# A causal five-tap convolution in 64x64 quadrants instead of shifted copies, in an attention and gated-unit kernel

## The chip, the cores and the metric

The kernel runs on one core of a Trainium2 chip. The metric is the device time of one execution in microseconds (us). A core has five engines that run side by side and wait for each other only through semaphores: TensorE (PE, matrix products into PSUM; PEld are its weight loads), VectorE (DVE), ScalarE (ACT), GpSimd (POOL) and SyncE (SP), which here only issues transfers. Sixteen DMA engines move the data.

## The reference

Attention over chosen chunks of keys, followed by a gated linear unit. For 4 batches, 8 heads, 768 positions and head size 64:

```python
k_min, k_max = k_chunks.min(3), k_chunks.max(3)         # 24 chunks of 32 keys
ub = sum_d max(q*k_min, q*k_max)                        # a bound for each query and chunk
ub = where(chunk is not later than the query's, ub, -1e9)
top = the 6 chunks with the largest ub
scores = where(key in a chosen chunk and not later than query, q@k.T / 8, -1e9)
x = softmax(scores) @ v          # then x is [4, 768, 512], heads side by side
gate = sigmoid(sum_k conv_w[k] * x shifted by 4-k positions)   # 5 taps, each channel alone
out = (gate * (x @ w_val)) @ w_out
```

## The kernel before, in words

Two heads make a pair, 128 channels; there are 16 pairs, four to a batch. Every pair goes through the same stages, in two halves of 384 positions where a PSUM bank (512 floats to a partition) asks for it:

- `load`: K, Q and V of the pair, in float32, rows of 64 floats. `tr` transposes K and Q on TensorE (L462), `kev` and `qev` copy them to float16 (`Kh`, `Qh`).
- `kred` takes the maximum and minimum over each chunk, `ksmall` (L493 to L499) makes the small matrix `KB` from them: the chunk values less those of the first chunk, in a high and a low float16 part, each head in its own half of the partitions. `KB` is zeroed once, by the operations `kbz`, so that one head's columns don't meet the other's rows.
- `qlo` makes the low part of Q; `rhi` and `rlo` the positive parts. `ub` (L547) sums four products for each of five blocks of 128 queries, 96 columns each: 24 chunks, two heads, two terms.
- `bsum`, `top`, `cmp` find the sixth largest bound and mark what is below it, `selT` transposes the marks (L587), `mcopy` copies them to `MT`.
- `score` (L606, L611) multiplies keys and queries of the two heads in the two halves of the array's rows, and adds the penalty for chunks not chosen; `exps` (L620) takes the exponential, `tri` (L628) clears what is above the diagonal.
- `av` (L649) multiplies by V with a column of ones, `norm` divides, `toxT` (L674) transposes the result and `xcopy` stores it as `xT`: channels on partitions, positions along the row with four zeros before.
- the convolution. `xw` (L684) writes `xT` to a scratch area in DRAM as 32 rows of four channel groups, and `xs` (L690) reads it back four times into `XS`, two of the four copies shifted by three positions. A partition of `XS` then holds a channel of every group, and `conv` (L707) makes 32 channels at a time, three column offsets with weights `WD`, in four column strips of the array, the four copies serving for the taps and for the high and low part of the weights. The last pair doesn't go through DRAM: it takes ten full matmuls a half with diagonal weights `WF` (L700). `w_split` and `w_diag` make `WD`, `l_split` and `l_diag` make `WF`, on VectorE and GpSimd, in the start.
- `tanh` (L713) makes the gate, and at the end of a batch `val` (L732), `gated` (L740), `outmm` (L756), `outev` (L766, L763) and `outdma` make the output.

The order of the work is written out before anything runs. `graph` lists all operations with the engine, an assumed duration, what they read and write and which PSUM banks they hold; `Graph.schedule` plays this through and, on an engine that is free, starts the ready operation with the smallest key:

```python
def key(stage, p, x=0.0):
    return p * period + off[stage] + off.get((stage, p), 0.0) + x
```

The offsets `OFF` (by stage) and `DELTA` (by stage and pair) set the priorities. The order that comes out is the order of the instructions on each engine, and each engine keeps it on the chip, so an instruction that waits holds up those behind it on its engine. SyncE issues loads, scratch transfers and output in one such queue. `NBUF` says how many buffers a stage has; `XS` has three of 6,192 B a partition.

Of the kernel before, what the change touches and what calls it, by code (L numbers as in the profile page):

```python
# [47 lines left out]
for _bi, _segs in enumerate(BANKS):  # L48
    for _col, _jt, _q0, _n in _segs:
        for _i in range(_n // 128):  # L50
# [3 lines left out]
            MT=2, on=2, xT=8, XS=3, g=8, gv=8, osb=4, scr=4)  # L54

PERIOD = 13.8602
OFF = dict(wbig=1148.236, cw=125.765, load=358.845, ktr=-336.423, qtr=-37.679, kev=406.626, qev=-139.346,
           ksm=-456.212, spl=623.116, vc=107.062, ub=-495.797, top=132.081, selT=-719.785, sc=-163.548,
           ex=-132.526, av=74.786, nrm=-290.402, tox=-288.094, xs=-175.045, conv=-212.494, tanh=-65.208,
           val=282.113, gv=294.749, out=-225.697, ev=-231.055)  # L60
# [3 lines left out]

DELTA = dict(
    wbig=(-4.147, -9.138, 14.054, 16.549, 24.22, 23.981, -3.255, -6.784, -8.585, -2.745, 13.034, 0, -24.136,
        -9.796, 0, 3.457),
    cw=(0, 89.865, 2.841, 1.73, -0.853, 3.445, 0, 7.465, 3.491, 0, -27.97, 1.384, -15.849, 36.25, -0.166,
        -20.384),
    load=(2.212, 2.245, 11.447, 7.343, 5.77, 0, 21.497, 8.567, -0.48, -11.783, -22.651, -40.845, -3.315,  # L70
        -5.727, -1.703, -8.004),
    ktr=(0, -2.634, 4.621, 8.626, 0.714, 0, 7.232, -2.689, -0.185, 4.209, -4.073, 0, 4.296, 0, 15.148, -5.02),
    qtr=(-15.204, 1.215, 0.818, 1.874, -8.456, -4.665, 3.458, -9.187, -23.627, 0.086, -14.556, 178.494, -3.223,
        14.633, -145.093, 7.271),
    kev=(11.876, -5.688, -9.671, 8.56, -7.116, 0, 12.665, 0.619, -15.123, -13.007, -10.166, -6.817, 6.199,
        -3.806, -0.155, -1.266),
    qev=(37.149, 2.471, -16.182, 10.459, 29.657, -0.249, -3.69, 9.604, -0.818, 2.696, -1.078, 12.98, -4.017,
        5.163, 5.476, 5.435),
    ksm=(0, -4.38, 5.046, 9.366, -11.093, -1.908, 3.385, -3.157, -13.805, 2.514, -0.981, 0, 1.21, 4.081,
        11.674, 10.127),  # L80
    spl=(0.346, -24.171, -2.279, -4.139, -5.56, -6.293, 12.646, 0.444, 0, -3.044, 0.73, 2.081, -5.907, -1.059,
        -2.827, -3.273),
    vc=(17.191, 3.409, 9.445, 3.878, -0.963, 0.335, 1.042, -2.48, 4.91, 5.77, 4.98, -4.793, 2.229, -17.202,
        -0.574, -2.167),
    ub=(13.662, 0, 0, 0, -8.33, -0.206, 0, 3.499, 3.993, -0.744, -2.331, 15.574, 26.827, 28.804, 16.738, 22.841),
    top=(25.292, -24.694, 4.497, -2.001, 1.256, 0, 16.093, 20.425, 0.505, -0.792, 0.187, 5.136, 4.425, 0.403,
        15.388, 11.54),
    selT=(-1.809, 13.447, 1.899, 2.153, -2.029, 27.133, 0.995, -4.451, -1.013, 1.728, 3.47, 2.835, 5.548,
        -1.394, -3.599, -4.491),
    sc=(-9.568, -6.679, 5.526, 4.615, -3.539, -11.917, -0.459, -1.374, 9.815, -3.896, 14.566, -29.319, 8.563,  # L90
        30.742, -5.263, -5.85),
    ex=(-15.686, -3.542, 41.162, 0, 8.566, 12.219, 4.858, -2.833, -10.993, 3.823, 16.222, 17.001, 13.392,
        -7.227, -1.623, -6.598),
    av=(-5.142, 0, -0.433, 0, 2.631, -5.212, 0, -5.273, 3.957, -3.38, 21.214, 11.344, 0.382, 2.169, -2.023,
        -2.85),
    nrm=(3.682, -5.189, 0, 0.178, -1.097, -13.888, 0, 4.991, 1.934, 0.324, 17.742, 0, 0, 0, 2.094, 5.151),
    tox=(0, 0.806, -0.064, 4.178, 10.744, -13.609, -5.142, -5.072, 0.301, 13.148, 1.471, -2.4, 16.567, 3.615,
        10.288, 0),
    xs=(0.835, -6.145, 0, -2.707, -15.901, -3.535, -0.514, 15.609, -2.935, -5.898, -7.227, -6.339, -7.872,
        2.836, -17.515, -1.283),  # L100
    conv=(1.109, -9.317, -7.864, 1.674, 14.425, 10.565, -18.213, 12.768, -35.205, -0.311, 0.911, -3.335, 4.553,
        0.715, -2.444, -81.052),
    tanh=(2.328, -10.547, 0.619, -51.267, -16.342, 0, 1.062, 25.583, 15.578, 4.988, -1.56, -26.423, -22.742,
        -18.959, 4.891, 1.516),
    val=(6.813, -1.57, 4.188, 7.508, 0, -26.519, -2.852, -6.757, 6.641, -4.111, -1.579, 0.052, 10.772, 5.618,
        -1.442, 3.684),
    gv=(2.408, -10.058, -23.155, -50.121, -16.673, -7.413, -28.068, -2.821, 0, -0.313, -1.153, 5.876, 2.097,
        5.659, -0.953, -3.286),
    out=(2.159, -7.291, 5.362, -0.981, 12.886, 0, -0.946, 13.16, 0, 18.939, 0.187, 0, 4.861, 24.141, 16.05,
        24.703),  # L110
    ev=(0.036, 2.704, 13.217, 11.95, 16.092, 5.482, 5.301, 2.521, -1.154, -11.056, -34.733, -21.796, -10.2,
        19.865, -1.415, 6.277),
# [163 lines left out]
def act(n):  # L276
    return 0.051 + n / 1200.0
# [14 lines left out]
def graph(off, period, nbuf):  # L292
# [34 lines left out]
    def c_zero(i):  # L327
        return lambda: t.nc.vector.memset(t.tiles["KB"][i], 0.0)
    for i in range(2):
        G.op(f"kbz{i}", "DVE", 0.2, -190, c_zero(i), w=[("KBz",)])  # L330
# [37 lines left out]
    def w_cw():  # L368
        t.nc.sync.dma_start(out=t.cw, in_=t.conv_w.rearrange("k (c d) -> (k c) d", d=32))
    G.op("cw", "SP", 0.6, key("cw", 1), w_cw, w=[("cw",)], lat=3.0)  # L370
# [6 lines left out]
    def w_rep():  # L377
        t.nc.vector.tensor_copy(out=t.cw4, in_=t.cw.unsqueeze(2).to_broadcast([80, 32, 4]))
    G.op("cwrep", "DVE", 0.6, 11.4, w_rep, r=[("cw",)], w=[("cw4",)])

    def w_tr():
        t.nc.tensor.transpose(out=bank("cwT")[:, 0:80], in_=t.cw4.rearrange("p d b -> p (d b)"),
                              identity=t.ident[0:80, 0:80])
    G.op("cwT", "PE", 0.12, 11.4, w_tr, r=[("cw4",), ("ident",)], ps=["cwT"])

    def w_split():
        nc, b = t.nc, bank("cwT")
        v, c4 = nc.vector, t.ident.rearrange("p (c b) -> p c b", b=4)
        v.tensor_reduce(out=t.pm[:, 0:4], in_=t.ident.rearrange("p (c b) -> p b c", b=4), axis=AX.X, op=ALU.add)
        v.tensor_reduce(out=t.id4, in_=c4, axis=AX.X, op=ALU.add)  # L390
        v.tensor_tensor(out=t.pm[:, 4:6], in0=t.pm[:, 0:2], in1=t.pm[:, 2:4], op=ALU.add)
        v.tensor_tensor(out=t.pm[:, 6:7], in0=t.pm[:, 0:1], in1=t.pm[:, 1:2], op=ALU.add)
        v.tensor_tensor(out=t.pm[:, 7:8], in0=t.pm[:, 2:3], in1=t.pm[:, 3:4], op=ALU.add)
        v.tensor_copy(out=t.whi, in_=b[:, 0:80])
        v.tensor_tensor(out=t.wlo, in0=b[:, 0:80], in1=t.whi, op=ALU.subtract)
        v.tensor_scalar(out=t.wlo, in0=t.wlo, scalar1=t.pm[:, 5:6], scalar2=None, op0=ALU.mult)
        v.scalar_tensor_tensor(out=t.wlo, in0=t.whi, scalar=t.pm[:, 4:5], in1=t.wlo, op0=ALU.mult, op1=ALU.add)
        v.tensor_scalar(out=t.wsel, in0=t.wlo[:, 0:48], scalar1=t.pm[:, 6:7], scalar2=None, op0=ALU.mult)
        v.scalar_tensor_tensor(out=t.wsel[:, 0:32], in0=t.wlo[:, 48:80], scalar=t.pm[:, 7:8], in1=t.wsel[:, 0:32],
                               op0=ALU.mult, op1=ALU.add)  # L400
    G.op("wsplit", "DVE", 2.7, 11.4, w_split, r=[("cwT",), ("ident",)], w=[("wsel",)], ps=["cwT"],
         after=[G.ops[-1]])

    def w_diag(j):
        def emit():
            sl = slice(12 * j, 12 * j + 12)
            t.nc.gpsimd.tensor_tensor(
                out=t.WD[:, sl, :], in0=t.id4.unsqueeze(1).to_broadcast([128, 12, 32]),
                in1=t.wsel[:, sl].unsqueeze(2).to_broadcast([128, 12, 32]), op=ALU.mult)
        return emit  # L410
    for j in range(4):
        G.op(f"wdiag{j}", "POOL", 0.8, 12.3 + 0.1 * j, w_diag(j), r=[("wsel",)], w=[("WD",)])


    def l_dma():
        t.nc.sync.dma_start(out=t.cl, in_=t.conv_w[:, DM - 128:DM])
    G.op("cl", "SP", 0.5, key("cw", 3), l_dma, w=[("cl",)], dma=0.1)

    def l_tr():
        t.nc.tensor.transpose(out=bank("clT")[:, 0:KSZ], in_=t.cl, identity=t.ident[0:KSZ, 0:KSZ])  # L420
    G.op("clT", "PE", 0.1, key("cw", 5), l_tr, r=[("cl",), ("ident",)], w=[("clT",)], ps=["clT"])

    def l_split():
        v, b = t.nc.vector, bank("clT")
        v.tensor_copy(out=t.lh, in_=b[:, 0:KSZ])
        v.tensor_copy(out=t.lw[:, 0:KSZ], in_=t.lh)
        v.tensor_tensor(out=t.lw[:, KSZ:2 * KSZ], in0=b[:, 0:KSZ], in1=t.lh, op=ALU.subtract)
# [480 lines left out]
```

The softmax here doesn't subtract the row's maximum and nothing guards it: scores larger than these inputs give would overflow.

## Time and profile before

| | |
|---|---|
| time, median of 3 runs | 226.72 us (225.72 to 227.03) |
| span of the profiled execution | 226.8 us |
| mean granted TensorE clock | 0.932 |
| PE, DVE, ACT, POOL busy | 86%, 68%, 63%, 44% |
| moved by DMA | 41.53 MB, 183 GB/s |
| XS<-scr | 60 transfers of 193.3 KB |
| scr<-xT | 15 transfers of 193.5 KB |
| K, Q, V | 80 transfers, 18.4 MB |

The page gives busy time by engine, the span in 40 slices (a digit is tenths; PEclk is the clock that TensorE was granted), the chain of work that ended last, the costliest groups of instructions by line and shape, and the transfers. Other views answer for a stretch of time: busy time by stretch, the chain or the instructions in order of time, and who waited for whom. A busy share alone doesn't tell what a change is worth; the chain and the stretches do.

### The profile page before, as it was taken

What the parts mean: (1) busy time and instruction counts of PE and PEld (TensorE: products, weight loads), DVE (VectorE), ACT (ScalarE), POOL (GpSimd) and SP (SyncE); (2) the same over time, 40 slices, a digit from 0 to 9 for tenths busy, and PEclk for the clock granted to TensorE, in tenths of its full rate; (3) what the DMA queues carried; (4) which work ended last, traced back from release to release, by engine and by line L of the source; (5) the groups of instructions that cost most, each with busy time, mean ns of one, the idle gap of its engine ahead of it and who ended that gap; (6) DMA issues with size and microseconds to landing.
All of it is one profiled execution on the core that took longest, in us unless ns stands there. A gap on an engine that the chain in (4) does not pass through costs nothing.

```text
span 226.8 us, 7127 instructions
## 1 busy us (share of the span) xinstructions
PE 195.6 (86%) x2710; PEld 131.4 (58%) x2710; DVE 155.1 (68%) x495; ACT 141.9 (63%) x310; POOL 99.1 (44%) x219
## 2 busy tenths in 40 slices
PE   7355999999995899993999996986999999939993
PEld 2255777858664768561586783562665658515441
DVE  4989899979986388985198896694576547203252
ACT  2313796996996458695589943793899881231421
POOL 8799886487183324358047613443163410000000
PEclk9857699999999589999699999997999999997999
DMA  5999998788858996898599699787143007674333
GB/s 122 220 218 219 151 208 175 176 179 238 218 137 195 242 269 139 193 265 281 131 211 254 154 231 260 160 281 251 35 143 134 9 7 198 197 259 150 139 137 140
DMA packets 84519, 41.53 MB, mean 183 GB/s; under 512 B 76545, under 2 KB 79494, under 8 KB 84486
## 3 DMA queue, kind: packets, MB, share of 16 engines
q1 hardware_dynamic: 83430, 40.04, 72.1%
q0 software_dynamic: 1056, 1.05, 3.1%
q8 instruction: 21, 0.34, 0.6%
q14 instruction: 12, 0.10, 0.1%
HBM read 32.86 MB, written 9.26 MB: 186 GB/s over the span
## 4 chain that ended last, share of the span: by engine, by line
PE 63%; DMA 11%; DVE 7%; POOL 5%; SPq 5%; ACT 4%; issue 2%; ACTq 0%; DVEq 0%; POOLq 0%
DMA XS<-scr 9%; PE b L732 8%; PE b L606 8%; PE b L756 8%; PE b L649 8%; PE b L707 8%; PE b L462 7%; PE b L611 6%; SPq L690 5%; PE b L547 5%; ACT P L620 4%; POOL WF L433 3%; PE b L587 2%; PE b L674 2%; DMA qn<-in_q_dram 2%
## 5 line engine op out<-in xcount | busy, mean ns | idle before, releaser
L620 ACT ACTIVATE P<-b 128x512 f16<-128x512 f32 (+2 forms) x192 | 89.8, 598 | 17.0 <-PE b L611 12.0
L628 POOL TENSOR_SCALAR_AFFINE_SELECT P<-P 128x512 f16<-128x512 f16 (+1 forms) x64 | 34.4, 557 | 39.3 <-ACT P L620 38.5
L606 PE MATMUL b<-Qh,Kh 64*128 64x128 f16 (+3 forms) x384 | 41.0, 267 | 0.1
L611 PE MATMUL b<-MT,E 64*128 64x128 f16 (+4 forms) x352 | 37.5, 263 | 0.0
L474 DVE TENSOR_REDUCE km<-b 128x12 f32<-128x384 f32 x64 | 32.8, 549 | 3.6 <-PE b L462 2.8
L740 DVE SCALAR_TENSOR_TENSOR gv<-g,b 128x384 f16<-128x384 f32 x32 | 17.5, 550 | 24.2 <-PE b L732 21.7
L707 PE MATMUL b<-XS,WD 128*32 128x384 f16 x360 | 20.5, 364 | 13.2 <-DMA XS<-scr 12.9
L713 ACT ACTIVATE g<-b 128x384 f32<-128x384 f32 x32 | 15.3, 503 | 24.0 <-PE b L707 15.8
L649 PE MATMUL b<-VA,P 128*128 128x65 f16 x672 | 29.1, 198 | 0.0
L649 PEld LDWEIGHTS <-P 128*128 128x128 f16 x672 | 26.0, 100 | 3.7 <-issue 1.9
L606 PEld LDWEIGHTS <-Kh 64*128 64x128 f16 x384 | 18.5, 96 | 13.6 <-issue 8.9
L732 PE MATMUL b<-xT,wval 128*128 128x384 f16 x128 | 24.8, 332 | 0.0
L504 ACT ACTIVATE Qh<-b 128x384 f16<-128x384 f32 x32 | 15.9, 548 | 12.6 <-PE b L462 12.3
L766 ACT ACTIVATE osb<-b 128x512 f32<-128x512 f32 x21 | 12.9, 613 | 16.6 <-PE b L756 16.4
L536 POOL CAST VA<-vn 128x768 f16<-128x768 f32 x16 | 13.3, 838 | 22.3 <-DMA vn<-in_v_dram 11.6
L756 PE MATMUL b<-wout,gv 128*128 128x512 f16 x96 | 22.7, 379 | 0.0
L468 ACT ACTIVATE Kh<-b 128x384 f16<-128x384 f32 x32 | 16.0, 545 | 9.8 <-PE b L462 8.7
L707 PEld LDWEIGHTS <-WD 128*32 128x32 f16 x360 | 9.1, 103 | 21.8 <-issue 15.7
L611 PEld LDWEIGHTS <-E 64*128 64x128 f16 x352 | 17.7, 97 | 4.2 <-issue 1.1
L462 PE MATMUL b<-ident,qn 128*128 128x128 f32 x96 | 17.0, 308 | 3.0 <-DMA qn<-in_q_dram 3.0
L462 PE MATMUL b<-ident,kn 128*128 128x128 f32 x96 | 15.5, 301 | 4.7 <-DMA kn<-in_k_dram 2.8
L658 DVE TENSOR_TENSOR on<-b,rcp 128x384 f16<-128x384 f32 x32 | 17.8, 558 | 1.1
(82 smaller groups left out, 328.9 us busy)
## 6 DMA issues: line engine op xcount, KB each, us to landing
XS<-scr SPq DMA_DIRECT2D x60, 193.3 KB
kn<-in_k_dram SPq DMA_DIRECT2D x32, 192.0 KB
qn<-in_q_dram SPq DMA_DIRECT2D x32, 192.0 KB
vn<-in_v_dram SPq DMA_DIRECT2D x16, 384.0 KB
out_dram<-osb SPq DMA_DIRECT2D x24, 256.0 KB
scr<-xT SPq DMA_DIRECT2D x15, 193.5 KB
wval<-in_moe_w_val_dram POOLq DMA_DIRECT2D x1, 512.0 KB, 8.1
wout<-in_moe_w_out_dram POOLq DMA_DIRECT2D x1, 512.0 KB, 10.5
```

The costliest lines, as they stand in the source:

```text
L462: t.nc.tensor.transpose(out=b[:, j * 128:(j + 1) * 128], in_=vv(name, p)[:, 3 * w + j, :], identity=t.ident)
L474: t.nc.vector.tensor_reduce(out=vv("km", p)[:, i, w * 12:(w + 1) * 12], in_=bank(("kn", p, w))[:, 0:HB].rearrange("p (c t) -> p c t", t=CH ...
L606: nc.tensor.matmul(out=bb[hh][:, col:col + n], lhsT=kh[HP[hh], jt * 128:(jt + 1) * 128], rhs=qh[HP[hh], q0:q0 + n], start=(si == 0), stop= ...
L611: nc.tensor.matmul(out=bb[hh][:, col + m0 - q0:col + n], lhsT=t.E[HP[hh], jt * 128:(jt + 1) * 128], rhs=mt[HP[hh], m0 - 128:q0 + n - 128], ...
L620: t.nc.scalar.activation(out=t.P[p % 2][hh][bi], in_=bank(("s", p, bi, hh))[:, 0:n], func=AF.Exp, scale=0.125 / QS)
L628: t.nc.gpsimd.affine_select(out=ap, in_=ap, pattern=[[0, n], [1, 128]], compare_op=ALU.is_ge, fill=0.0, base=0, channel_multiplier=-1)
L649: t.nc.tensor.matmul(out=b[:, qt, :], lhsT=t.P[p % 2][hh][bi][:, col:col + 128], rhs=vv("VA", p)[:, hh, jt, :], start=(jt == 0), stop=(jt ...
L658: t.nc.vector.tensor_tensor(out=vv("on", p)[:, :, hh * 64:(hh + 1) * 64], in0=b[:, :, 0:D], in1=rc.unsqueeze(2).to_broadcast([128, NT, D]) ...
L707: t.nc.tensor.matmul(out=b[32 * g:32 * g + 32, 0:HB], lhsT=t.WD[:, o * 16 + (p % 4) * 4 + g, :], rhs=x[:, g * XW + w * HB + o:g * XW + w * ...
L732: t.nc.tensor.matmul(out=k[:, 0:HB], lhsT=t.wval[:, ct, et * 128:(et + 1) * 128], rhs=t.xT[:, (4 * b_ + ct) % 8, 4 + w * HB:4 + (w + 1) * HB],
L740: t.nc.vector.scalar_tensor_tensor(out=vv("gv", 4 * b_ + et)[:, sl], in0=vv("g", 4 * b_ + et)[:, sl], scalar=1.0, in1=bank(("val", b_, et, ...
L756: t.nc.tensor.matmul(out=k, lhsT=vv("gv", 4 * b_ + et)[:, s * 128:(s + 1) * 128], rhs=t.wout[:, et, :], start=(et == 0), stop=(et == NCT - 1))
```

## The change

The convolution is done in quadrants of the array. A quadrant multiplies 64 channels (half of the partitions) by a 64x64 diagonal weight and writes 64 channels. The two halves of positions are computed at the same time: the first half of the rows (channels 0 to 63 of `xT`) makes positions 0 to 383 and the second half of the rows (channels 64 to 127) makes positions 384 to 767. For what remains, a copy `XQ` of `xT` has the two halves of the partitions swapped. Ten steps (five taps, high and low part of the weight) of four matmuls make a pair, all of them one operation that holds both PSUM banks. Two transfers inside SBUF make `XQ`; scratch area and shifted copies are gone, and the last pair is treated like the others. The weights `WQ` are built in the start, from conv_w as 40 rows of 64, in place of `WD` and `WF`.

The bounds stream only chunks that a block of queries can see: of the four products the first keeps all 24 chunks and clears the bank, the others take 4i+8 (i is the block's number). `ksmall` works on both heads at once, with a mask `hm` that also carries the scale, so `KB` is written whole and isn't zeroed in advance.

In the start, TensorE's planned gaps before 26 us are filled with products of a zero tile (`fill`), and for pairs 0 and 1 `rhi` and `mcopy` go from VectorE to ScalarE.

Assumed transfer times in the planner, PERIOD, OFF and DELTA change too, so the order of all stages is another one. `val` must come after the convolution of its channels.

```diff
-            MT=2, on=2, xT=8, XS=3, g=8, gv=8, osb=4, scr=4)
+            MT=2, on=2, xT=8, XS=3, XQ=3, g=8, gv=8, osb=4, scr=4)
+EARLY = (0, 1)
+FILL, FILL_MM = 26.0, 0.3
+CONV = "QQQQQQQQQQQQQQQQ"
...
-            t.nc.vector.memset(t.tiles["KB"][i], 0.0)
+            t.nc.vector.memset(t.hm[HP[hh], hh, :], QS)
+            t.nc.vector.memset(t.hm[HP[hh], 1 - hh, :], 0.0)
...
+        def q_diag(k):
+            def emit():
+                for m in range(2):
+                    t.nc.gpsimd.tensor_tensor(
+                        out=t.WQ[:, m, k], in0=t.id2.unsqueeze(1).to_broadcast([128, 8, 64]),
+                        in1=t.qw[:, m, 8 * k:8 * k + 8].unsqueeze(2).to_broadcast([128, 8, 64]), op=ALU.mult)
...
-            e.tensor_scalar(out=ks, in0=ks, scalar1=QS, scalar2=None, op0=ALU.mult)
-            for hh in range(2):
-                hp, cs = HP[hh], slice(hh * NCH, (hh + 1) * NCH)
-                e.tensor_copy(out=kb[hp, :, 0, cs], in_=ks[hp])
-                e.tensor_tensor(out=kb[hp, :, 1, cs], in0=ks[hp], in1=kb[hp, :, 0, cs], op=ALU.subtract)
+            e.tensor_tensor(out=kx, in0=ks.unsqueeze(2).to_broadcast([128, 2, 2, NCH]),
+                            in1=t.hm.unsqueeze(1).to_broadcast([128, 2, 2, NCH]), op=ALU.mult)
+            e.tensor_copy(out=kb[:, :, 0], in_=kx)
+            e.tensor_tensor(out=kb[:, :, 1], in0=kx, in1=kb[:, :, 0], op=ALU.subtract)
...
-                    t.nc.tensor.matmul(out=b[:, i * 96:(i + 1) * 96], lhsT=lhsT,
-                                       rhs=kb[:, m].rearrange("p a c -> p (a c)"), start=(k == 0), stop=(k == 3))
+                    n = NCH if k == 0 else 4 * i + 8
+                    t.nc.tensor.matmul(out=o[:, :, 0:n], lhsT=lhsT,
+                                       rhs=kb[:, m].rearrange("p l s c -> p (l s) c")[:, :, 0:n],
+                                       start=(k == 0), stop=(k == 3))
...
+        def swap(p=p):
+            for i in range(2):
+                t.nc.sync.dma_start(out=vv("XQ", p)[HP[1 - i], :], in_=t.xT[HP[i], p % 8, :])
...
+        def convq(p=p):
+            for k in range(2 * KSZ):
+                for x, d in ((t.xT[:, p % 8, :], 0), (vv("XQ", p), 1)):
+                    for r in range(2):
+                        c = r ^ d
+                        a = r * HB + k % KSZ
+                        t.nc.tensor.matmul(out=bank(("cv", p, r))[HP[c], 0:HB],
+                                           lhsT=t.WQ[HP[r], k // KSZ, k % KSZ, (p % 4) * 2 + c, :],
+                                           rhs=x[HP[r], a:a + HB], start=(k == 0), stop=(k == 2 * KSZ - 1))
...
-                     r=[("xT", 4 * b_ + ct) for ct in range(4)] + [("wbig",)], w=[("val", b_, et, w)],
+                     r=[("xT", 4 * b_ + ct) for ct in range(4)] + [("wbig",), ("cv", 4 * b_ + et, w)], w=[("val", b_, et, w)],
...
+        if o.eng == "PE" and last is not None and o.start < FILL:
+            a, b = last.start + last.occ, o.start
+            n = int((b - a - 0.15) / FILL_MM)
+                def emit(n=n, k=free[0]):
+                    for _ in range(n):
+                        t.nc.tensor.matmul(out=t.psb[k], lhsT=t.warm[:, 0:128], rhs=t.warm, start=True, stop=True)
```

## The prediction

> **What bounds the kernel now.** I read the page first (busy shares, the 40 slices), then the chain that ended last, then busy time by stretches, then the timeline at the points that these name.
>
> ```profile
> PE 195.6 (86%) x2710; PEld 131.4 (58%) x2710; DVE 155.1 (68%) x495; ACT 141.9 (63%) x310; POOL 99.1 (44%) x219
> PE   7355999999995899993999996986999999939993
> PEclk9857699999999589999699999997999999997999
> DMA  5999998788858996898599699787143007674333
> ```
>
> TensorE is the engine nearest to its limit, with a slow start (slices 2 to 4 at clock 5 to 7) and holes near slices 13, 19, 25 and 36. The DMA engines are near full until about slice 28.
>
> ```profile
> PE 63%; DMA 11%; DVE 7%; POOL 5%; SPq 5%; ACT 4%; issue 2%; ACTq 0%; DVEq 0%; POOLq 0%
> 102.27 5.74 DMA XS<-scr
> 108.25 2.11 PE b L707 x18
> 203.83 2.11 PE b L707 x24
> ```
>
> The chain is TensorE for 63% and DMA for 11%; of the latter the load of the shifted copies (XS) alone has 9.5% of the span, 21.6 us, and its issue (SPq L690) another 4.8%, 10.9 us. In time order the holes are XS loads of 4 to 6 us, and the convolution after one runs at half speed, 2.11 us instead of 1.10.
>
> ```profile
> 0.00:27.60 27.60, 17.90 (x137) 12.47 (x137) 22.50 (x79) 9.56 (x19) 24.01 (x47) 0.75 1.13 186
> 27.60:69.20 41.60, 40.93 (x682) 30.18 (x684) 38.11 (x130) 36.93 (x85) 27.29 (x65) 1.00 0.85 189
> 69.20:83.00 13.80, 9.98 (x132) 8.00 (x130) 7.46 (x18) 6.28 (x15) 3.32 (x6) 0.75 0.97 241
> 97.00:111.00 14.00, 9.33 (x132) 5.30 (x130) 7.05 (x24) 8.99 (x20) 8.12 (x19) 0.90 0.90 242
> 134.00:156.00 22.00, 17.28 (x272) 11.30 (x273) 15.07 (x52) 13.27 (x28) 8.91 (x22) 1.00 0.90 240
> 156.00:191.00 35.00, 34.99 (x549) 22.48 (x542) 21.41 (x65) 27.13 (x60) 10.11 (x22) 0.95 0.29 88
> 191.00:205.00 14.00, 10.50 (x91) 5.74 (x93) 2.98 (x7) 3.77 (x7) 0.00 (x0) 0.96 0.74 239
> ```
>
> Columns: stretch, length, busy us (instructions) of PE, PEld, DVE, ACT, POOL, clock, DMA share, GB/s. A good stretch issues some 16 matmuls a us; 69 to 83 and 97 to 111 issue 9.5. Because matmul ends are modelled, I priced the work instead. The timeline gives the step from one group's start to the next at full clock: 0.67 us for 6 transposes, 0.86 for the 20 bounds matmuls, 0.28 for 5 mask transposes, 0.0528 each for score and mask matmuls (46 in some 2.43), 0.0345 for P times V, 0.06 for the output transposes, 1.10 for 24 convolution matmuls, 0.1625 for `val`, 0.22 for `out`. Counting each line's matmuls in each stretch and multiplying gives 170.8 us of work in 226.8, so 56.0 lost:
>
> - 0 to 27.6: work 8.4, lost 19.2
> - 27.6 to 69.2: 35.9, lost 5.7
> - 69.2-83, 97-111 and 134-156: 31.1 in 49.8, lost 6.7 + 6.5 + 5.5 = 18.7
> - 83-97, 111-134, 156-191: 68.6 in 72.0, lost 3.4
> - 191 to the end: 26.9 in 35.8, lost 8.9
>
> ```profile
> 83.41 1.17 PE L707 MATMUL b<-XS,WD 128*32 128x384 f16 x24
> 84.51 0.28 PE L606 MATMUL b<-Qh,Kh 64*128 64x256 f16 x2
> 8.84 3.20 POOL L407 TENSOR_TENSOR WD<-id,wsel 128x384 f16<-128x384 f32 x4 [1.12 <-DVE wsel L399]
> 12.02 6.25 POOL L433 TENSOR_SCALAR WF<-identh,lw 128x128 f16<-128x128 f16 x10
> 21.63 0.20 PE L547 MATMUL b<-KB,rh 128*128 128x96 f16 x1 [2.38 <-POOL KB L499]
> ```
>
> The first two lines give the convolution's price: 24 matmuls, four column strips at a time, are six steps of 384 columns; 1.10 us is 6 x 0.160 plus 0.14 on the change of mode. The last three show GpSimd building convolution weights for 9.45 us in the start, with the bounds of pair 1 behind it.
>
> **What the Trainium skill says.** "TensorE: Matmul & The Clock Gate", Part 3, has matmuls in disjoint tiles of the array run together, 10.6 times for 16 tiles of 32x32. The trace shows each half: two 64-row score matmuls of 512 columns advance in 0.22 us, four column strips in 0.16. Rows and columns split at once is in no row here. "TensorEngine Tiling (Array Packing)", Key Properties: a change of mode drains the array; the 0.14 us agrees. Its Restrictions say that column tiling disables Fast Weight Load; the clock-gate page's LDWEIGHTS section then prices a load at columns/1.2 ns, 53 ns for 64 columns. Part 1 of that page says that the array runs at half clock until busy for some 3.4 us; the 0.75 of the first stretch, and 6 transposes in about 1.5 us there against 0.67 later, agree.
>
> **The change part by part.**
>
> *Convolution.* Per pair 24 matmuls become 40 (10 taps, hi and lo, by 4 quadrants) of 384 columns, four together: 10 x 0.160 + 0.14 = 1.74 us if the loads hide. If they don't, 40 x 53 ns = 2.1 us, estimated from the skill's price. I take 1.75: today's loads are hidden, and neighbours in the new order lie in different rows and columns. Fifteen pairs gain 0.65 each, +9.75 us; the last pair's 20 full matmuls (3.26 us to the next group) go to 1.75, -1.5.
>
> *Copies.* Gone are 60 XS loads and 15 writes, 75 x 193 KB = 14.5 of 41.5 MB, and the round trip through DRAM. In come 32 copies of 64 rows of 1,548 B, 0.2 MB a pair, 3.2 MB. SyncE issues 2 instead of 5 DMAs a pair, so saves some 1.8 us of issue (0.59 each), and no longer waits for the write (9.4 us) with K/Q/V loads queued behind it. No row has an on-chip copy; between 2 us (the skill's fixed DMA cost, "DMA: Bandwidth & Descriptors", Anatomy) and the 4 to 6 us of XS I take 2.5 us, hidden in the middle by other pairs' matmuls. The queued xT wait remains.
> The stretches with XS holes lost 18.7 us. I keep 2.0, for loads that still come late: 256 B rows of K, Q, V are most of the 76,545 small packets and stay.
>
> *Bounds.* Of four matmuls per tile three shrink from 96 columns to 32, 48, 64, 80 and 96. Price 43 ns at 96; the nearest narrow row, 65 columns, steps 34.5. Saved 3 x (3 x 8.3 + 5) = 0.09 us a pair, -1.4 in all. Short runs in the streamed operand I cost at nothing; no row shows them.
>
> *Work after:* 170.8 + 9.75 - 1.5 - 1.4 = 177.7 us.
>
> *Start.* VectorE is busy 22.5 of 27.6 us. It loses the weight split (about 2.9 us, 5.96 to 8.7), the cast chain (1.0), the KB memsets, and to ScalarE (9.6 busy, so free) two `rh` (0.4 to 0.96) and two mask copies (0.49); it gains about 1.3 us of small operations. Net about 5 us, ahead of pair 0's mask. GpSimd gets no relief: 10 weight products of 512 elements at the 830 ns per 384 of L407 are 1.1 us each, 11 us, against 9.45. ksmall goes from seven instructions (2.2 us from its rows) to five wider ones, about 1.6 to 2.4; I count nothing. The pair-1 bounds stay behind it, which hold up pair 1, not pair 0. The filler matmuls keep the clock up, worth up to 2 us (three sets of 6 transposes at 1.5 against 0.67); if a filler runs at half clock (0.43 us in the warm-up against its 0.3 in the plan) real matmuls queue behind it. Together I take 4 us: 19.2 to 15.2.
>
> *27.6 to 69.2* loses 5.7 with VectorE and ScalarE both at about 90%; I take 4.6, since a pair's mask is ready earlier.
>
> *End.* The 8.9 holds the 3.3 us from 200.5 to 203.8 and 1.0 of slow convolution after it; these go, 4.6 stay. The last pair now waits for its swap, beside `val` and `out`.
>
> *val's new dependence on cv*, and one convolution holding two PSUM banks: the wait on PE blocks everything behind it, but the planner can put other pairs' matmuls before it; I cost it at nothing and keep 3.0 of the 3.4 in the smooth stretches.
>
> Sum: 177.7 + 15.2 + 4.6 + 2.0 + 3.0 + 4.6 = 207.1 us.
>
> **The rivals.**
> - *The weight loads show* (18%): conv 2.2 us a pair, 16 x 0.45 = +7, so 214. For: 64 columns are twice today's 32, and Fast Weight Load is off. Against: today's loads leave no gap.
> - *The holes close and the new order packs* (15%): DMA holes and smooth losses fall to 1 together, the start to 13.7, the middle to 4: 177.7 + 13.7 + 4 + 1 + 4 = about 200.5. For: 83 to 97 lost only 0.1 us in 14. Against: GpSimd is no lighter in the start.
> - *Holes move* (2%): late loads, convolutions that wait for swaps and PSUM take the place of XS, and the added 7 us of PE work cancels the rest: 226.7.
> - *Quadrants don't run together* (7%): two at a time, 20 x 0.16 = 3.2 us a pair, +1.45 x 16 = 23 us more TensorE work, with the better start kept: 230; one at a time is far worse. For: no row of this trace combines both splits. Against: each half is shown.
> - Forecast, 207: 58%.
>
> **How the numbers follow.** Slower by over 0.5% is the last rival, 0.07; within 0.5% is the one before, 0.02; all else, 0.91, is faster. The low end, 199, is a little below the packed case; the high end, 216, takes in the exposed loads. Outside are 9% above and some further tail at both ends.
>
> **What would show it.** Right: no XS line in the chain, TensorE over 90% of the chain's middle, the DMA volume near 30 MB, a group of 40 convolution matmuls stepping 1.75 us, scores of pair 0 starting before 22 us (24.1 now), clock near 1.0 in the first 27 us. Wrong: convolution groups of 2.1 us or more (loads), of 3.2 (quadrants one after another), holes ended by the swap copy or by K/Q loads of 3 us and more, or a start still ended by GpSimd's weights.

## The result and the profile after

The changed kernel takes 207.15 us (207.04 to 208.03, four runs), the kernel before in the same session 226.88 us (225.72 to 227.43). The ratio is 0.9145, with an interval of 0.9101 to 0.9189. Here and below, an execution more than 1.5% above the fastest of its kernel counts as slow and is left out of the ratio, while medians and ranges keep it. The span of the profiled execution is 206.3 us at a mean clock of 0.979. A span is some 1.8 us shorter than the time of the same execution: this one took 208.03 us and the other three have spans of 205.3 to 205.4; the profiled execution of before, with its span of 226.8, took 228.62 us and so was longer than the median of before. TensorE runs 2,994 matmuls in it, for 2,710 before.

The page of the changed kernel, the lines that answer to those shown of before:

```profile
PE 193.2 (94%) x2994; PEld 132.7 (64%) x2994; DVE 153.8 (75%) x481; ACT 141.8 (69%) x316; POOL 90.3 (44%) x185
...
PE   7909999999999999999989999999999999999991
...
PEclk9985999999999999999999999999999999999998
DMA  5999969617998989788997400310400430133344
...
PE 78%; DVE 11%; ACT 5%; issue 3%; POOL 1%; ACTq 0%; DVEq 0%
...
XQ<-xT SPq DMA_DIRECT2D x32, 96.8 KB, 2.2
```

The holes of TensorE near slices 13, 19, 25 and 36 are gone; one slow place is left, slice 3, and with it one dip of the clock, to 5 in slice 4. DMA doesn't stand in the chain any more (11% before). A copy into `XQ` lands after 2.2 us. The page's volume is 29.88 MB, for 41.53.

Four of the stretches shown of before (length, busy us and instructions of PE, PEld, DVE, ACT, POOL, clock, DMA share, GB/s):

```profile
0.00:27.60 27.60, 20.24 (x146) 12.47 (x148) 20.36 (x53) 10.76 (x23) 21.17 (x39) 0.88 1.02 231
27.60:69.20 41.60, 40.90 (x773) 31.53 (x770) 38.72 (x133) 36.19 (x84) 26.75 (x55) 1.00 0.80 168
69.20:83.00 13.80, 13.77 (x237) 9.20 (x237) 11.81 (x46) 10.89 (x26) 4.71 (x10) 1.00 0.95 217
97.00:111.00 14.00, 13.36 (x233) 9.18 (x229) 10.33 (x43) 10.30 (x23) 5.93 (x13) 1.00 0.96 231
```

The two stretches that issued 9.5 matmuls a microsecond now issue 17. Priced as in the prediction, with 1.75 us for a pair's convolution and 0.69 for a pair's bounds, the changed kernel has 175.1 us of work and 31.2 lost. By stretch the loss is, with the forecast behind it: 0 to 27.6, 20.1 (15.2); 27.6 to 69.2, 3.1 (4.6); 69.2 to 191, 3.7 (2.0 and 3.0); from 191 to the end, 4.2 (4.6). So the start did not gain what was forecast, and the rest of the kernel made up for it.

The convolution in the chain of the changed kernel (start, us, what), a single pair and two pairs back to back:

```profile
61.85 1.75 PE b L790 x40
...
123.61 3.38 PE b L790 x80
```

A pair takes 1.75 us alone and 1.69 in a double group. The four quadrants advance together, 0.162 us per step, and no gap for weights shows between them. Two steps of the single pair, from the timeline of TensorE:

```profile
62.30 0.33 PE L790 MATMUL b<-xT,WQ 64*64 64x384 f16 x2
62.30 0.33 PE L790 MATMUL b<-XQ,WQ 64*64 64x384 f16 x2
62.46 0.33 PE L790 MATMUL b<-xT,WQ 64*64 64x384 f16 x2
62.47 0.33 PE L790 MATMUL b<-XQ,WQ 64*64 64x384 f16 x2
```

What went wrong in the start stands in the timeline of VectorE (start, us, instruction) and of GpSimd in the changed kernel. First VectorE:

```profile
8.88 1.03 DVE L539 TENSOR_TENSOR km<-km 128x24 f32<-128x24 f32 x1
9.95 0.99 DVE L540 TENSOR_TENSOR ks<-km 128x48 f32<-128x48 f32 x1
10.97 1.02 DVE L541 TENSOR_TENSOR kx<-ks,hm 128x96 f32<-128x96 f32 x1
12.02 0.93 DVE L543 CAST KB<-kx 128x96 f16<-128x96 f32 x1
12.99 1.01 DVE L544 TENSOR_TENSOR KB<-kx,KB 128x96 f16<-128x96 f32 x1
```

Then GpSimd:

```profile
7.83 10.73 POOL L451 TENSOR_TENSOR WQ<-id,qw 128x512 f16<-128x512 f32 x10
22.87 0.75 POOL L539 TENSOR_TENSOR km<-km 128x24 f32<-128x24 f32 x1 [4.30 <-DVE km L519]
```

The five small instructions of pair 0 (`ksmall`) take 1.0 us each, one after another for 5.1 us, while GpSimd makes the ten weight products. In the kernel before, the seven that they replace took 0.17 to 0.34 us each, 1.8 us in all, although GpSimd was making `WF` beside them:

```profile
12.14 0.17 DVE L493 TENSOR_TENSOR km<-km 128x24 f32<-128x24 f32 x1
...
13.34 0.34 DVE L498 CAST KB<-ks 64x48 f16<-64x48 f32 x1
13.72 0.20 DVE L499 TENSOR_TENSOR KB<-ks,KB 64x48 f16<-64x48 f32 x1
```

TensorE's wait for this matrix of pair 0, in total, times and longest, in the kernel before (L499) and in the changed kernel (L544), where it is the longest wait of TensorE:

```profile
PE b L547 <- DVE KB L499: 1.5, 1, 1.5
PE b L605 <- DVE KB L544: 3.9, 1, 3.9
```

The scores of pair 0 began at 23.50 us, where they had begun at 24.1. The bounds of pair 1 began at 26.60 us, where they had begun at 21.63.

### The profile page after: what moved, and what is told of

Same layout as the page of the kernel before. It is cut to its first block, busy times and chain, and to the rows that moved or that the text cites. A ratio compares the mean times of both kernels' runs of the same rounds, so it can differ in the third digit from the quotient of the medians.

```text
span 206.3 us, 7533 instructions
## 1 busy us (share of the span) xinstructions
PE 193.2 (94%) x2994; PEld 132.7 (64%) x2994; DVE 153.8 (75%) x481; ACT 141.8 (69%) x316; POOL 90.3 (44%) x185
## 2 busy tenths in 40 slices
DMA packets 82165, 29.88 MB, mean 145 GB/s; under 512 B 75986, under 2 KB 79058, under 8 KB 82130
## 4 chain that ended last, share of the span: by engine, by line
PE 78%; DVE 11%; ACT 5%; issue 3%; POOL 1%; ACTq 0%; DVEq 0%
PE b L790 12%; PE b L844 10%; PE b L711 10%; PE b L820 10%; PE b L668 9%; PE b L507 9%; PE b L673 7%; PE b L605 5%; ACT P L682 4%; PE b L736 3%; DVE ql L557 2%; PE b L646 2%; DVE km L519 2%; PE b L332 2%; DVE rl L575 1%
## 5 line engine op out<-in xcount | busy, mean ns | idle before, releaser
L682 ACT ACTIVATE P<-b 128x512 f16<-128x512 f32 (+2 forms) x192 | 87.5, 594 | 4.8 <-PE b L673 3.4
L668 PE MATMUL b<-Qh,Kh 64*128 64x128 f16 (+3 forms) x384 | 38.1, 258 | 0.0
L673 PE MATMUL b<-MT,E 64*128 64x128 f16 (+4 forms) x352 | 35.8, 255 | 0.1
L790 PE MATMUL b<-xT,WQ 64*64 64x384 f16 x320 | 28.1, 324 | 0.0
L790 PE MATMUL b<-XQ,WQ 64*64 64x384 f16 x320 | 28.1, 324 | 0.0
L711 PE MATMUL b<-VA,P 128*128 128x65 f16 x672 | 27.2, 194 | 0.2 <-ACT P L682 0.2
L711 PEld LDWEIGHTS <-P 128*128 128x128 f16 x672 | 24.2, 98 | 4.4 <-issue 2.1
L668 PEld LDWEIGHTS <-Kh 64*128 64x128 f16 x384 | 17.8, 94 | 12.5 <-issue 8.0
L828 DVE SCALAR_TENSOR_TENSOR gv<-g,b 128x384 f16<-128x384 f32 x32 | 17.6, 550 | 9.1 <-ACT osb L854 5.5
L790 PEld LDWEIGHTS <-WQ 64*64 64x64 f16 x640 | 17.7, 106 | 9.2 <-issue 2.5
L720 DVE TENSOR_TENSOR on<-b,rcp 128x384 f16<-128x384 f32 x32 | 17.8, 557 | 1.1
L605 PE MATMUL b<-KB,rh 128*128 128x96 f16 x80 | 12.5, 209 | 5.1 <-DVE KB L544 3.9
L557 DVE SCALAR_TENSOR_TENSOR ql<-b,Qh 128x256 f16<-128x256 f32 (+1 forms) x32 | 14.6, 482 | 2.9 <-ACT Qh L549 2.7
```

Source lines behind the costliest of these rows:

```text
L557: t.nc.vector.scalar_tensor_tensor(out=vv("ql", p)[:, a - 128:a - 128 + n], in0=bank(("qn", p, w))[:, a - w * HB:HB], scalar=QS, in1=vv("Q ...
L605: t.nc.tensor.matmul(out=o[:, :, 0:n], lhsT=lhsT, rhs=kb[:, m].rearrange("p l s c -> p (l s) c")[:, :, 0:n], start=(k == 0), stop=(k == 3))
L668: nc.tensor.matmul(out=bb[hh][:, col:col + n], lhsT=kh[HP[hh], jt * 128:(jt + 1) * 128], rhs=qh[HP[hh], q0:q0 + n], start=(si == 0), stop= ...
L673: nc.tensor.matmul(out=bb[hh][:, col + m0 - q0:col + n], lhsT=t.E[HP[hh], jt * 128:(jt + 1) * 128], rhs=mt[HP[hh], m0 - 128:q0 + n - 128], ...
L682: t.nc.scalar.activation(out=t.P[p % 2][hh][bi], in_=bank(("s", p, bi, hh))[:, 0:n], func=AF.Exp, scale=0.125 / QS)
L711: t.nc.tensor.matmul(out=b[:, qt, :], lhsT=t.P[p % 2][hh][bi][:, col:col + 128], rhs=vv("VA", p)[:, hh, jt, :], start=(jt == 0), stop=(jt ...
```

## The experiments

Every kernel is the changed one with the edit that is shown. The kernel before was measured beside each group and came to 224.7 to 226.9 us; the ratios below are to those runs. Versions that lie close together are compared by their own times: the changed kernel, run again as `z0_after`, gave the same 207 us.

**The changed kernel again.**

> The changed kernel as it is, to have it beside the others on this chip: 207 us, within 0.5%.

It took 207.0 us (206.97 to 207.47), a ratio of 0.9269 (0.9227 to 0.9312) to a before that came to 224.7 in that group. The median repeats to 0.1%, so the ratio moved because of the kernel before. The five small instructions ran from 8.26 to 12.99 us, again at 0.93 to 1.02 each for the last four. The scores of pair 0 begin at 22.49 us in this profile, and 21.5 us are lost up to 42 us, where the first profile of the same kernel has 23.50 and 22.3. A difference of 1 us between the starts of two kernels therefore says nothing.

**The shifted copies back, everything else as changed.**

```diff
-CONV = "QQQQQQQQQQQQQQQQ"
+CONV = "SSSSSSSSSSSSSSSD"
```

> The changed kernel with the convolution alone taken back: fifteen pairs through the shifted copies, the last by full diagonals, under the new keys. Theory (the gain is the removed holes, less the added TensorE work): TensorE work falls by about 8 us, the DMA volume is back near 41 MB, TensorE waits for XS again, 214 to 224 us. Rival (the new order of all stages brings the gain, the shifted copies were only badly placed before): within 2% of 207, waits for XS under 5 us.

218.19 us (215.29 to 220.66), ratio 0.9621 (0.9467 to 0.9775). As the theory had it, with 41.53 MB moved again. The two runs that make the ratio average 216.4 us. In the chain of its profiled execution, which was the longest of its four runs (span 218.9) and is read for what is in it and not for its size, the loads of the copies are back, for instance:

```profile
146.11 3.54 DMA XS<-scr
```

So in this order some 9 of the 20 us (216.4 for 207.1) hang on the way of the convolution alone, although quadrants give TensorE more work.

**The new operations in the old order.** PERIOD, OFF and DELTA of the kernel before, with the new operations:

```diff
-PERIOD = 12.3221
+PERIOD = 13.8602
...
-           gv=141.487, out=-125.43, ev=-151.26)
+           gv=294.749, out=-225.697, ev=-231.055)
```

> The changed operations under the period and keys of the kernel before. Theory (the gain is in the operations: no XS holes, whatever the order): 207 to 214. Rival (the new keys carry the gain): 219 or more, with new holes on TensorE.

212.12 us (211.22 to 213.09), ratio 0.9493 (0.9423 to 0.9563). In the same group the kernel before came to 224.7 and the changed kernel to 207.0, so the operations carry some 12.6 us and the new order some 5, of which 3 to 4 show in the profiled spans (209.5 for 206.3 and 205.6). No DMA is in its chain either, and its line of TensorE shows where these are:

```profile
PE   7729978999999999999999999999999999999991
```

Priced by stretch it loses 19.3 to 27.6 us and 6.0 from there to 69.2, where the changed kernel loses 20.1 and 3.1; the rest differs by 1 us. The better second stretch is therefore the order's doing. The scores of pair 0 begin at 21.11 us here, earlier than in the changed kernel, and the kernel is slower all the same.

**All chunks in the bounds** (the order kept):

```diff
-                    n = NCH if k == 0 else 4 * i + 8
+                    n = NCH
```

> The four bounds products stream all 24 chunks again; nothing else and no order changes. Theory (TensorE bound, a step of 25 to 27 ns for the narrow ones): 0.17 us for each of 16 pairs, +2.7 us, about 210. Rival (TensorE has slack where the bounds lie): 207, within 0.5 us.

208.92 us (208.62 to 209.04), ratio 0.9287 (0.9213 to 0.9361): 1.8 us more. The four runs here and the ten of the changed kernel don't overlap. In the changed kernel the 20 matmuls step 0.69 us (85.08 to 85.77), against 0.86 before; 16 pairs are 2.7 us, of which two thirds reach the end. The narrow ones, up to 64 columns, step some 27 ns. The first of them in the timeline of the changed kernel:

```profile
85.08 0.20 PE L605 MATMUL b<-KB,rh 128*128 128x96 f16 x1
85.12 0.18 PE L605 MATMUL b<-KB,rl 128*128 128x32 f16 x1
85.15 0.18 PE L605 MATMUL b<-KB,Qh 128*128 128x32 f16 x1
85.17 0.18 PE L605 MATMUL b<-KB,ql 128*128 128x32 f16 x1
```

The start of one matmul to the start of the next is the step: 0.04 us for 96 columns, 0.02 to 0.03 for 32. The short runs in the streamed operand cost nothing that can be seen.

**No filler** (the order kept):

```diff
-FILL, FILL_MM = 26.0, 0.3
+FILL, FILL_MM = 0.0, 0.3
```

> No filler products in TensorE's early gaps; the order is the same. Theory (the start is set by VectorE's and GpSimd's chain, not by TensorE's clock): lower clock in the first 27 us, time up by less than 1 us. Rival (the clock sets the start): scores of pair 0 start 1.5 us later or more, time +2 us.

208.87 us (208.32 to 209.44), ratio 0.9287 (0.9207 to 0.9367): 1.7 us more, nearer to the rival's number, though not by its mechanism. The scores of pair 0 begin at 23.04 us, no later than with filler. The clock is what changed, in the line of the page and in the first stretch:

```profile
PEclk9955599999999999999999999999999999999999
```

```profile
0.00:27.60 27.60, 16.71 (x103) 10.81 (x104) 18.42 (x50) 9.92 (x21) 21.65 (x40) 0.69 1.04 236
```

At 0.69 instead of 0.88 TensorE does 6.7 us of priced work by 27.6 us instead of 7.5. The filler doesn't hurry pair 0, whose chain runs through VectorE; what it changes is the clock at which the matmuls of this stretch run.

**The convolution with half its steps.** The low parts of the weights are left out, so TensorE has 16 x 0.81 = 13 us less to do:

```diff
-            for k in range(2 * KSZ):
+            for k in range(KSZ):
```

> Leaves out the low parts of the convolution's weights: 20 quadrant products a pair in place of 40, the same order. Theory (TensorE bound, quadrants run four together at 0.16 us): 5 x 0.162 us less a pair, -13 us, about 194. Rival (VectorE, ScalarE or the loads are right behind TensorE): less than half of that is gained, 200 or more.

197.82 us (197.37 to 199.0), ratio 0.8803 (0.8724 to 0.8883): 9.3 us less, not 13. Its chain shows who takes over:

```profile
PE 62%; DVE 26%; ACT 4%; issue 3%; DMA 2%; POOL 1%; SPq 0%; ACTq 0%; DVEq 0%
```

VectorE goes from 11% of the chain to 26%. TensorE is the bound of the changed kernel, and VectorE is close behind.

**No early help from ScalarE.** `rhi` and `mcopy` of pairs 0 and 1 back on VectorE, the order planned anew:

```diff
-EARLY = (0, 1)
+EARLY = ()
```

> The positive part of Q and the mask copy of pairs 0 and 1 back on VectorE; the planner makes the order anew, so later stages move a little too. Theory (VectorE sets the start beside GpSimd): 0.4 to 1 us for each on the way to pair 0's mask, scores of pair 0 some 1 us later, 207.5 to 209. Rival (GpSimd's weights alone set the start): 207, within 0.5 us.

213.62 us (213.02 to 216.65), ratio 0.9459 (0.9384 to 0.9534), far more than expected. Pair 0's scores begin at 23.64 us and the first stretch loses 20.3, as in the changed kernel; 27.6 to 69.2 loses 6.6 instead of 3.1 and the rest 1.3 us more. What its TensorE waited for (us in total, times, longest):

```profile
PE b L605 <- DVE rh L571: 4.9, 1, 4.9
```

The bounds of a pair wait once for `rh` for 4.9 us. Neither the theory nor the rival had expected that. But the planner changed the order everywhere, so this run doesn't give the value of the two moves by themselves.

**The weight products out of VectorE's way.** Now to the start. An extra operation `gate` on GpSimd reads pair 0's `KB`, and the products come after it, all ahead of pair 1's `ksmall`:

```diff
+    def gate():
+        kb = t.tiles["KB"][0]
+        t.nc.gpsimd.tensor_tensor(out=t.gate, in0=t.kx[0][:, 0, 0, 0:1], in1=kb[:, 0, 1, 0, 0:1], op=ALU.subtract)
...
-    order = fill(G, order, t)
+    order = late(fill(G, order, t), t, {"ksm1": (0, 1, 2, 3, 4)})
```

> GpSimd builds the convolution's weights only after pair 0's small bounds matrix is written (a GpSimd instruction of one column that reads the matrix goes ahead of them); all other instructions keep their order. Theory (VectorE's five small instructions for pair 0 take 5.1 us because they run beside GpSimd's weight products): alone they take 0.2 us each, about 1.2 us in all, the scores of pair 0 start near 20 us instead of 23.5, time 3 to 4 us less, 203.5. Rival 1 (they are slow for another reason): still about 1 us each, 207. Rival 2 (the weights, finished some 2.5 us later, hold up pair 1's matrix instead): short instructions, but less than 1 us gained.

206.45 us (206.0 to 207.88), ratio 0.9249 (0.9194 to 0.9304), against 207.0 of `z0_after` in the same group. The timeline of VectorE has the five instructions at full speed:

```profile
7.87 0.18 DVE L539 TENSOR_TENSOR km<-km 128x24 f32<-128x24 f32 x1
...
8.62 0.21 DVE L543 CAST KB<-kx 128x96 f16<-128x96 f32 x1
8.87 0.26 DVE L544 TENSOR_TENSOR KB<-kx,KB 128x96 f16<-128x96 f32 x1
```

They take 1.3 us in place of 5.1, and pair 0's scores begin at 17.59 us in place of 23.50. And yet the medians differ by only 0.55 us, and the ranges overlap: the second rival's result. The timeline of GpSimd of the same kernel tells why:

```profile
9.43 11.47 POOL L451 TENSOR_TENSOR WQ<-id,qw 128x512 f16<-128x512 f32 x10
20.86 0.23 POOL L539 TENSOR_TENSOR km<-km 128x24 f32<-128x24 f32 x1
```

Pair 1's small matrix now stands behind 11.5 us of products. TensorE's wait of 3.9 us for the matrix of pair 0 is gone, and it waits for that of pair 1 instead:

```profile
23.26 0.20 PE L605 MATMUL b<-KB,rh 128*128 128x96 f16 x1 [2.81 <-POOL KB L544]
```

**The products split.** Three of the five pairs of products ahead of pair 1's `ksmall`, the rest later between the masks:

```diff
-    order = fill(G, order, t)
+    order = late(fill(G, order, t), t, {"ksm1": (0, 1, 2), "vc3": (3,), "tri3.50": (4,)})
```

> The same, and the last two of the five weight operations moved further back on GpSimd, behind its work for the first pairs and ahead of the first convolution. If pair 1's matrix was held up in the version before, another 1 to 2 us less, 202; if not, the same as it, or up to 1 us more where the weights now hold up masks of the first pairs.

206.15 us (205.44 to 207.61), ratio 0.9231 (0.9175 to 0.9288). Pair 1's small matrix starts at 18.30 us; up to 42 us 19.7 are lost, for 22.3 and 21.5 in the two profiles of the changed kernel. The total follows by less than 1 us. Part of the reason is that two of the products moved back, at 33.85 us, now stand before a mask of the first pairs, and TensorE waits for it:

```profile
37.03 0.71 PE L711 MATMUL b<-VA,P 128*128 128x65 f16 x17 [1.97 <-POOL P L690]
```

**The products by pair of heads, one tile.** A product makes all taps of two of the eight channel blocks (640 elements; the text below says 1,280), so that pair 0 needs only its own:

```diff
+                        out=t.WQ[:, m, :, 2 * g:2 * g + 2, :],
...
+    order = late(fill(G, order, t), t, "qdiag0", {"ksm1": ("qdiag0", "qdiag1")},
+                 {"vc5": ("qdiag2", "qdiag3", "wbig")})
```

> The convolution's weights in four groups, one for each pair of a batch, 2 products of 1,280 elements each, instead of ten products of 512: the first two groups after pair 0's bounds matrix, the last two, and the load of the big weights, behind GpSimd's work for pair 5's V; the rest keeps its order. Theory (the start is now bound by GpSimd, which has weights and the issue of the big loads ahead of masks and V copies of the first pairs): pair 1's matrix no later than in the split version (near 18 us), no weight products between 18 and 40 us, 2 to 3 us less than the changed kernel, 204 to 205. Rival (ScalarE's exponentials and VectorE bind once pair 0 is early, so GpSimd's relief buys nothing more): within 0.5 us of the split version's 206.2.

212.54 us (210.79 to 213.24), ratio 0.94 (0.9352 to 0.9447): a miss. It loses only 17.8 us up to 42, but 9.8 from 42 to 94 where the changed kernel loses 1.0. The first convolution doesn't wait for weights: it runs from 47.76 to 51.0 us, and the products of pairs 2 and 3 from 50.19 to 55.9. The load of `val`'s weights had been put behind these products, and TensorE waits for it:

```profile
62.70 1.46 PE L822 MATMUL b<-xT,wval 128*128 128x384 f16 x4 [4.04 <-DMA wval<-in_moe_w_val_dram]
```

The clock is at 0.5 from 62 to 68 us. Before that the bounds of a pair wait 1.59 us for an `rl` that runs beside the products.

**The same in four tiles**, the loads of the large weights ahead of the last two groups:

```diff
-        t.WQ = tl("WQ", [128, 2, KSZ, 8, 64], F16)
+        t.WQ = [tl(f"WQ{g}", [128, 2, KSZ, 2, 64], F16) for g in range(4)]
...
+                 {"tri2.01": ("wbig",), "tri3.01": ("qdiag2",), "vc5": ("qdiag3",)})
```

> As the version by pairs, but each group of weights has its own tile, so a convolution waits only for its own pair's weights; the load of the big weights goes behind pair 2's triangle masks, the third group behind pair 3's first two, the fourth behind pair 5's V. Theory (the version by pairs had 17.8 us lost up to 42 us against 22.3 for the changed kernel, and gave it back in waits for weights and the big load, 2.3 + 7.5 us against 1.0 from 42 to 94 us): the early gain stays, 202.5 to 204. Rival (loads of K, Q and V are the next bound, so an earlier start only waits for them): 206 or more, with waits on DMA between 42 and 94 us.

206.29 us (204.45 to 207.31), ratio 0.9162 (0.911 to 0.9214): the rival's number. Two stretches (columns as above):

```profile
0.00:27.60 27.60, 22.94 (x197) 14.29 (x198) 21.14 (x70) 14.98 (x34) 19.47 (x39) 0.94 1.17 200
42.00:55.00 13.00, 11.73 (x224) 9.37 (x221) 12.86 (x33) 8.72 (x21) 10.01 (x14) 1.00 1.07 205
```

By 42 us this kernel has lost 17.8, 4.5 less than the changed kernel (3.7 less than its repeat). Of this it gives back 2.5 from 42 to 55 us, where the changed kernel loses nothing: VectorE is busy for 12.86 of 13.0 us there. The timeline of VectorE shows the moved products at work, `NS` earlier and alone, and then beside the last products (50.31 to 53.04 us):

```profile
29.20 0.39 DVE L638 TENSOR_TENSOR NS<-mub,top 128x240 f16<-128x240 f32 x1
...
50.45 1.47 DVE L638 TENSOR_TENSOR NS<-mub,top 128x240 f16<-128x240 f32 x1
51.84 1.88 DVE L577 SCALAR_TENSOR_TENSOR rl<-Qh,ql 128x640 f16<-128x640 f16 x1
```

And the timeline of TensorE has the bounds behind that `rl`:

```profile
53.78 0.19 PE L607 MATMUL b<-KB,rl 128*128 128x32 f16 x1 [0.64 <-DVE rl L577]
```

So the weights take VectorE's time in these later places too, and there VectorE has none to spare. The rival had named late loads: one convolution did wait for its swapped copy, for 0.41 us. With another 0.5 us lost from 55 to 94, 1.5 of the 4.5 are left, and the span is 1.0 to 1.7 us shorter (204.6 for 205.6 and 206.3). This kernel differs from the one before it in two things, tiles and load. From 42 to 55 us it loses as much as that one (2.5 for 2.3), from 55 to 94 us 0.5 for 7.5; as the wait there was for the load, the earlier load explains the gain, and what separate tiles are worth isn't shown.

**Copies in place of products.** Each product on GpSimd replaced by two copies with one input. `WQ` is then full and not diagonal, so the gate is another one, with the same number and shapes of matmuls:

```diff
-                    t.nc.gpsimd.tensor_tensor(
-                        out=t.WQ[:, m, k], in0=t.id2.unsqueeze(1).to_broadcast([128, 8, 64]),
-                        in1=t.qw[:, m, 8 * k:8 * k + 8].unsqueeze(2).to_broadcast([128, 8, 64]), op=ALU.mult)
+                    for _ in range(2):
+                        t.nc.gpsimd.tensor_copy(
+                            out=t.WQ[:, m, k],
+                            in_=t.qw[:, m, 8 * k:8 * k + 8].unsqueeze(2).to_broadcast([128, 8, 64]))
```

> Each of the ten weight products on GpSimd (two inputs, 512 elements, 1.11 us) is replaced by two copies with one input of the same size; the instructions and their order are otherwise those of the changed kernel. The blocks of WQ are then full instead of diagonal, so the gate is another one; the shapes and the number of matmuls stay. Theory (it is the second input of GpSimd's products that holds up VectorE): the five small instructions of pair 0 take 0.2 to 0.3 us each instead of 1.0, and end near 9.2 us instead of 14.0; VectorE reaches pair 0's mask some 3.5 us sooner and the scores of pair 0 begin at 18 to 20 us instead of 23.5; the copies take 0.5 to 0.6 us each, 10 to 12 us in all; the time is 204 to 206. Rival 1 (any GpSimd work of that length and size beside it does it): small instructions 0.8 us or more, scores at 23 or later, 207. Rival 2 (broadcast float32 input read at that rate is what matters, a matter of degree): 0.4 to 0.7 us each.

205.72 us (205.59 to 206.12), ratio 0.9167 (0.9072 to 0.9261). The timelines of VectorE and of GpSimd in this kernel:

```profile
8.95 0.19 DVE L540 TENSOR_TENSOR km<-km 128x24 f32<-128x24 f32 x1
9.17 0.55 DVE L541 TENSOR_TENSOR ks<-km 128x48 f32<-128x48 f32 x1
...
10.48 0.50 DVE L544 CAST KB<-kx 128x96 f16<-128x96 f32 x1
11.02 0.69 DVE L545 TENSOR_TENSOR KB<-kx,KB 128x96 f16<-128x96 f32 x1
```

```profile
7.82 13.77 POOL L452 CAST WQ<-qw 128x512 f16<-128x512 f32 x20
```

The theory falls: one input holds VectorE up too, and the durations are those of the second rival. The hold is shorter, about in proportion: from the second on, the small instructions start 0.54 to 0.72 us apart beside copies of 0.69 us, and 0.97 to 1.07 apart beside products of 1.07. That is roughly one instruction of VectorE for each of GpSimd's. TensorE's wait for the matrix of pair 0 goes from 3.9 us to 1.6. Pair 0's scores begin at 21.10 us, later than expected, as the hold is only halved (2.8 us from the start of the five to their end, for 5.1), and pair 1's small matrix only at 21.56. The time is 1.3 us below that of the changed kernel, and the ranges don't overlap.

## Why the prediction was right, and where it wasn't

The time was forecast at 207.1 and came out at 207.15, with two of its terms wrong in opposite directions.

- *Convolution, +9.75 and -1.5.* Right: 1.75 us a pair, the quadrants together, no weight load in the open. The rivals with exposed loads and with quadrants one after another are out.
- *Copies.* Right: no XS and no DMA in the chain, 29.88 MB, 2.2 us to landing where 2.5 was taken. The 2 us that the prediction took from the Trainium skill ("DMA: Bandwidth & Descriptors", Anatomy of one DMA) are a fit to transfers issued from GpSimd; these are issued from SyncE. Putting the shifted copies back costs some 9 us.
- *Bounds, -1.4.* Too small a term: the pair saves 0.17 us and not 0.09. The 34.5 ns of the nearest row, 65 columns, was used as a price for narrower ones, which step some 27. Widening them again costs 1.8 us.
- *Start, "19.2 to 15.2".* The step that failed: 20.1 are lost, and the scores of pair 0 begin at 23.50 us (22.49 in the repeat) where less than 22 was to show it right. "ksmall goes from seven instructions (2.2 us from its rows) to five wider ones, about 1.6 to 2.4; I count nothing" was the wrong term: they took 5.1 us, because GpSimd's products ran beside them: with the products out of their way they took 1.3, beside copies 2.8. Those were counted as equally long as before, 11 us for 9.45, and as harmless to VectorE. The page "SBUF — State Buffer" of the Trainium skill, section "Who interferes with whom", states it: a VectorE instruction with two SBUF inputs contends with a GpSimd instruction that reads SBUF, and the loser is blocked for a whole instruction. The traces agree for the small instructions and the products, 1.0 us each beside them and 0.2 without (the fourth, a CAST, has one input, which that sentence doesn't cover, and was held as well). They don't agree everywhere: beside the single-scalar products of `WF` before the change, 0.63 us each, the same small two-input instructions took 0.17 to 0.21 us. What makes that difference was not tried. The profile of before had a sign of the hold. The same operation `rh` took three times as long where it ran into the last of the `WD` products (8.84 to 12.04 us):

```profile
11.26 0.96 DVE L526 TENSOR_SCALAR rh<-Qh 128x640 f16<-128x640 f16 x1
19.32 0.32 DVE L526 TENSOR_SCALAR rh<-Qh 128x640 f16<-128x640 f16 x1
```

  The prediction took this as a range, 0.4 to 0.96, and didn't ask for its cause.
- Nor would the forecast gain have followed from a quick pair 0. With pair 0's scores at 17.6 us only 0.55 us came off, since the products and pair 1's small matrix share GpSimd. The prediction put the pair-1 bounds behind GpSimd and took them to hold up pair 1 alone. In the changed kernel they begin 5.0 us later than before, and it is VectorE that pair 1's matrix waits for, with GpSimd idle for 4.3 us; once VectorE is free, GpSimd's products are what TensorE waits for. The orders that did best up to 27.6 us still lose 17.2 there, so the remaining 2.0 to the forecast 15.2 stay open.
- *The filler, "up to 2 us".* Right in size, 1.7 us, and through the clock, though the clock reached 0.88 and not 1.0. Without it the start would have been worse than before in clock, 0.69 for 0.75.
- *27.6 to 69.2, 5.7 to 4.6.* It fell to 3.1, and not because "a pair's mask is ready earlier": the scores of pair 0 begin 0.6 us earlier than before and the bounds of pair 1 5.0 us later. With the old keys it stays at 6.0. The new order did it; a change of keys alone had been given no term of its own, and it is worth some 5 us. The prediction had no way to price an order from the profile of another one.
- *69.2 to 191, 5.0.* 3.7 came out, and the end 4.2 for 4.6. Both about right; the order and the missing scratch traffic are not separated there.

With the start at 20.1 in place of 15.2, +4.9, the four other terms had to give it back: the work 2.6 less than forecast (1.3 of this the bounds), the second stretch 1.5, the rest 1.7. They sum to 5.8, which makes 206.2 of the forecast: the profiled span, 206.3. For the other 1.3 us of work, counting is enough: a matmul on the border of two stretches was counted in both, and over the whole span the same prices give 169.2 us before and 174.7 after.

The match to 0.1 us is luck, and in a second way too. The forecast was summed from stretches of a span, so 207.1 is a span and would be a time of some 208.9; three of the four executions have spans of 205.3 to 205.4. The sizes of the two largest terms, the convolution's matmuls and the XS waits, are not luck.

## What to carry to other kernels

A round trip through DRAM that only rearranges data may be worth replacing by more matmuls, if these keep the array's parts busy at the same time: here some 8 us more convolution on TensorE still came out some 9 us ahead of the copies. When a set-up is moved to an idle engine, look at what runs beside it on the engine that isn't idle: a "free" GpSimd held VectorE up by 4 us. And when the first unit of work is made faster, look at the second: with pair 0 five to six us earlier, TensorE waited 2.8 us for pair 1, and less than 1 us was left.

## What the runs showed of the hardware

- VectorE and GpSimd hold each other up without a semaphore between them, other than the start of this document has it. Small VectorE instructions (24 to 96 elements a partition) took 1.0 us each beside GpSimd's products of 1.07, 0.5 to 0.7 beside copies of 0.69, 0.2 alone. `NS`, 240 elements, went from 0.39 to 1.47 us and `rl` from 0.8 to 1.88 beside products of 1.36. It isn't seen everywhere: `rl` beside the products in the start took 0.82 us, and the small instructions beside the `WF` products of before 0.17 to 0.34.
- Four 64x64 quadrants with 384 columns advance in 0.162 us, the time of one full matmul of that width. A group takes some 0.14 us more than its steps (3.38 us for 20 of them, 1.75 for 10); that this is the change into the form was not tried by itself.
- A matmul of 32, 48 or 64 columns steps in some 27 ns, against 43 for 96: narrowing pays down to 64 columns, and below that nothing more was gained here.
